# A gated linear-attention kernel on one core: two neighbouring tokens per partition, and the order of the engines written out

## The chip, the cores and the metric

The kernel runs on one core of a Trainium2 chip. A core has TensorE (PE, whose weight loads are shown apart as PEld), VectorE (DVE), ScalarE (ACT), GpSimd (POOL) and SyncE (SP, which here only issues DMAs), all with their own in-order instruction streams, joined by semaphores. The metric is device time in microseconds; lower is better. Three runs of the kernel before took 164.64, 166.47 and 166.83 us, a median of 166.47 us.

## The reference

Inputs r, k, v, w have shape (batch 4, heads 8, tokens 768, head size 48) in float32, u is (8, 48). For each batch and head a 48 x 48 state is carried over the tokens, and the result feeds a token-mixing MLP with 384 = 8 x 48 features and 64 hidden ones:

```python
for t in range(S):
    cur = np.einsum('bhd,bhe->bhde', u[None] * kt, vt)          # bonus for the token itself
    y[:, :, t] = np.einsum('bhd,bhde->bhe', rt, state + cur)
    state = wt[:, :, :, None] * state + np.einsum('bhd,bhe->bhde', kt, vt)
# x: y with heads joined, (4, 768, 384)
W_tok = scale * np.einsum('bsd,btd->bst', x @ w_q, x @ w_k)
mixed = np.einsum('bst,btd->bsd', W_tok, x)
out = np.maximum(mixed, 0.0) @ w_out
```

## The kernel before

The work is cut into 12 units, three to a batch element; a unit is two chunks of 128 tokens. Each chunk has one token per partition, and the free dimension holds the 8 heads of 48. The scan over tokens becomes matrix products: inside a chunk, the logarithms of w are summed over tokens by a triangular matmul; exponentials of these sums scale r (up to the token) and k (inverse); scaled r and k are transposed, multiplied into a 128 x 128 matrix A for each head, masked to its strict lower part, and multiplied with v. A bf16 state (SB) carries over from chunk to chunk.

Three stages follow one another for each unit. `prep` (lines 136 to 169) loads (line 125, eight DMAs of 192 KB from the SP queue, in each of which a row is the 48 floats of one token and head, 192 bytes), takes the logarithm on ACT (L142), the sums on PE, two exponentials of 128 x 768 on ACT (L148, L156), the chunk decays (L158), the scaled r on DVE (`RdS`, L162), the scaled k on POOL (`KdS`, L164) and a bf16 copy of v on ACT (L167). `back` (171 to 203) transposes r and k on PE into `psT`, copies them out (`RKT`, L179), makes A on PE and the masked `AmB` on DVE (L189), the products r·u·k on POOL (L194, L197), their reduction on DVE (`diag`, L199) and the bonus-weighted values `Vd` on POOL (L201). `scan` (205 to 258) takes for each chunk the state (`Sn` on PE, `SB` on DVE, L226) and the output (`Y` on PE, `X` = Y + Vd on DVE, L238), then transposes X (`XT`, L247) and projects it (`qk`, L256, L257). After a batch element's third unit `moe` (260 to 283) does the rest: `Tps`, six `mps` with a Relu on ACT (L272), six `fps` of three matmuls each, copied out by DVE and ACT in turn (L280, L282) and stored from the ACT queue.

The program is written unit by unit, `prep` of a unit ahead of `back` and `scan` of the one before, and a scheduler in the framework reorders each engine's instructions. Tile pools set how far engines can run apart: loads have four buffers each; in PSUM the tags `big` (sums, `psT`, A), `s` (`Sn`, `Y`) and `m` (the MLP) have two each. All matmuls go through the helper on line 55.

Of the kernel before, what the change touches and what calls it, by code (L numbers as in the profile page):

```python
# [25 lines left out]
def kernel(  # L26
# [14 lines left out]
    C = 128  # L41
    NCH = S // C
    NP = H // 2
    NU = S // (2 * C)
# [9 lines left out]
    def mm(o, l, rr, start=True, stop=True, sgc=True, trans=False):  # L54
        nc.tensor.matmul(o, l, rr, start=start, stop=stop,  # L55
                         skip_group_check=sgc, is_transpose=trans)

    nc.scalar.preload_act_table_set("natural_log_exp_and_others")

    consts = ctx.enter_context(tc.tile_pool(name="consts", bufs=1))  # L60
    U128 = consts.tile([C, C], BF16, tag="U128")
    make_upper_triangular(nc, U128, 1.0, diag=True)
    US128 = consts.tile([C, C], BF16, tag="US128")
    make_upper_triangular(nc, US128, 1.0, diag=False)
    ID128 = consts.tile([C, C], BF16, tag="ID128")
    make_identity(nc, ID128)
    ones = U128[:, C - 1:C]

    iota0 = consts.tile([C, 1], mybir.dt.int32, tag="iota0")
    nc.gpsimd.iota(iota0, pattern=[[0, 1]], base=0, channel_multiplier=1)  # L70
    iota1 = consts.tile([C, 1], mybir.dt.int32, tag="iota1")
    nc.gpsimd.iota(iota1, pattern=[[0, 1]], base=1, channel_multiplier=1)
    bias_px = consts.tile([C, 1], F32, tag="bpx")
    bias_mi = consts.tile([C, 1], F32, tag="bmi")
    bias_c = consts.tile([C, 1], F32, tag="bc")
    nc.scalar.activation(bias_px, iota0, ACT.Copy, bias=0.0, scale=MU)
    nc.scalar.activation(bias_mi, iota1, ACT.Copy, bias=0.0, scale=-MU)
    nc.gpsimd.memset(bias_c, MU * C)


# [3 lines left out]
    for i in range(NB):  # L84
        for lst, nm, e in ((LW, "logw", nc.gpsimd), (RdS, "RdS", nc.vector),
                           (KdS, "KdS", nc.gpsimd)):
            t = consts.tile([C, 2, NP, C], BF16, name=f"{nm}{i}", tag=f"{nm}{i}")
            e.memset(t, 0.0)
            lst.append(t)
        t = consts.tile([C, 2, H], F32, name=f"pt{i}", tag=f"pt{i}")  # L90
        nc.vector.memset(t, 0.0)
        PT.append(t)
# [8 lines left out]
    ld = ctx.enter_context(tc.tile_pool(name="ld", bufs=4))  # L101
# [6 lines left out]
    mout = ctx.enter_context(tc.tile_pool(name="mout", bufs=4))  # L108

    def mtile(shape, dtype, name):  # L110
        return ps.tile(shape, dtype, name=name, tag="m", bufs=2)

    def stile(shape, dtype, name):
        return ps.tile(shape, dtype, name=name, tag="s", bufs=2)
# [4 lines left out]
    def load(n):  # L119
        b, m = divmod(n, NU)  # L120
        G = {}
        for nm, ap in (("w", w), ("k", k), ("r", r), ("v", v)):
            t = ld.tile([C, 2, H, D], F32, name=nm + "G", tag=nm + "G")
            for c in range(2):
                nc.sync.dma_start(out=t[:, c], in_=ap[  # L125
                    b, :, ds((m * 2 + c) * C, C)].rearrange("h p d -> p h d"))
            G[nm] = t
        return G

    def chd(t):  # L130
        return t
# [4 lines left out]
    def prep(n, G):  # L136
        P = {}
        logw = LW[n % NB]
        Rd = RdS[n % NB]
        Kd = KdS[n % NB]  # L140
        pt = PT[n % NB]
        nc.scalar.activation(pad(logw), chd(G["w"]), ACT.Ln, bias=0.0, scale=LN_SCALE)  # L142
        cw1 = big([C, 2, 512], F32, "cw1")
        lw4 = pad(logw)
        for c in range(2):
            mm(cw1[:, c, 0:DM].rearrange("p (h d) -> p h d", d=D), US128, lw4[:, c])
# [58 lines left out]
    def scan(n, P, st):  # L205
# [8 lines left out]
        for cc in range(2):  # L214
            c = 2 * m + cc
            SB = st["S"]
            if c + 1 < NCH:
                Sn = stile([C, DM], F32, "Sn")
                if SB is not None:
                    mm(Sn, ID128, SB, start=True, stop=False)  # L220
# [114 lines left out]
```

## Time and profile before

| | |
|---|---|
| profiled execution, whole | 165.66 us |
| its span, first to last instruction | 163.9 us |
| PE busy | 104.8 us in 1196 matmuls |
| DVE busy | 99.2 us |
| POOL busy | 95.7 us |
| ACT busy | 80.9 us |
| loads on the SP queue | 18.98 MB in 100242 packets |
| stores on the ACT queue | 4.72 MB in 3456 packets |

Times are of one profiled execution, in microseconds, and means of one instruction in nanoseconds. In the page's rows of 40 slices each digit is the busy share of a fortieth of the span in tenths; the DMA row is the mean over 16 DMA engines. A row of the groups reads: line, engine, operation, out<-in, shapes, count, then busy time and mean of one, then the idle time of the engine just before them and what ended it. A row of the timeline begins with start and duration. A matmul's listed length includes its passage through the array, so neighbours overlap; the pace is seen from the time from start to start.

### The profile page before, as it was taken

To read this page: it belongs to the slowest core of one execution; us is meant where nothing else is said; L and a number is where in the kernel's file an instruction comes from. 1 tells how busy PE (TensorE), PEld (TensorE's weight loads), DVE (VectorE), ACT (ScalarE), POOL (GpSimd) and SP (SyncE) were. 2 spreads that over 40 slices of the span, in tenths; PEclk is the share of its full clock that TensorE was granted. 3 is DMA by queue.
4 is the path that set the end of the run, shared out by engine and by line. 5 is a ranking of instruction groups with operands and counts; after the bars stand their busy time and mean duration, and the time that the engine had idled before them with its cause. 6 is when DMAs were issued, how large, how long until landed. Compare 5 with 4: busy or idle time off the path is not lost.

```text
span 163.9 us, 3082 instructions
## 1 busy us (share of the span) xinstructions
PE 104.8 (64%) x1196; PEld 70.8 (43%) x1196; DVE 99.2 (61%) x124; ACT 80.9 (49%) x152; POOL 95.7 (58%) x72
## 2 busy tenths in 40 slices
PE   0305103752379488994958898886589949857690
PEld 0203003441257365674637366665344527734240
DVE  4020203645668997899889978899582696670030
ACT  3535420430155576775729757793766342303721
POOL 7931009999994999598696952949960940000000
PEclk9999999999999999998799999699975995765967
DMA  5999999999999990289989969999970331000034
GB/s 111 194 187 187 190 187 186 182 210 172 192 183 190 167 175 0 72 221 268 194 165 190 174 173 256 220 197 187 159 140 0 110 125 59 4 0 0 0 127 161
DMA packets 104512, 24.23 MB, mean 148 GB/s; under 512 B 101041, under 2 KB 104498, under 8 KB 104498
## 3 DMA queue, kind: packets, MB, share of 16 engines
q1 hardware_dynamic: 100242, 18.98, 75.0%
q10 hardware_dynamic: 3456, 4.72, 8.2%
q0 software_dynamic: 800, 0.34, 1.7%
q8 instruction: 9, 0.15, 0.4%
q14 instruction: 5, 0.04, 0.1%
HBM read 19.66 MB, written 4.72 MB: 149 GB/s over the span
## 4 chain that ended last, share of the span: by engine, by line
PE 29%; SPq 16%; POOL 15%; DVE 14%; issue 10%; ACT 7%; DMA 6%; ACTq 0%; POOLq 0%
SPq L125 15%; DMA rG<-in_r_dram 6%; DVE AmB L189 6%; PE fps L55 6%; POOL uk L197 5%; PE Y L55 5%; POOL uk L194 4%; PE qk L55 3%; PE psT L55 3%; DVE RKT L179 3%; PE cw L55 3%; POOL KdS L164 3%; POOL Vd L201 3%; PE Tps L55 3%; ACT XT L247 2%
## 5 line engine op out<-in xcount | busy, mean ns | idle before, releaser
L164 POOL TENSOR_TENSOR KdS<-kG,emcw 128x768 bf16<-128x768 f32 x12 | 21.1, 1758 | 18.9 <-ACT emcw L156 11.1
L189 DVE TENSOR_TENSOR AmB<-A,US 128x1024 bf16<-128x1024 f32 x24 | 28.3, 1219 | 4.4 <-PE A L55 4.3
L162 DVE TENSOR_TENSOR RdS<-rG,ecwx 128x768 bf16<-128x768 f32 x12 | 17.2, 1433 | 14.5 <-DMA rG<-in_r_dram 13.4
L197 POOL TENSOR_TENSOR uk<-uk,rG 128x768 f32<-128x768 f32 x12 | 24.3, 2028 | 0.5
L201 POOL TENSOR_TENSOR Vd<-VB,diag 128x768 bf16<-128x768 bf16 x12 | 18.4, 1532 | 10.0 <-DVE diag L199 6.0
L194 POOL TENSOR_TENSOR uk<-kG,ubc 128x768 f32<-128x768 f32 x12 | 21.7, 1810 | 1.7 <-DMA kG<-in_k_dram 1.7
L179 DVE COPY RKT<-psT 128x2048 bf16<-128x2048 bf16 x12 | 14.6, 1218 | 11.1 <-PE psT L55 11.1
L247 ACT COPY XT<-xt_ps 128x768 bf16<-128x768 bf16 x12 | 9.6, 798 | 20.8 <-PE xt_ps L55 20.6
L238 DVE TENSOR_TENSOR X<-Y,Vd 128x384 bf16<-128x384 f32 x24 | 13.2, 552 | 9.2 <-PE Y L55 5.9
L55 PEld LDWEIGHTS <-KdS 128*128 128x128 bf16 x176 | 13.7, 113 | 11.5 <-POOL KdS L164 9.4
L55 PE MATMUL Y<-VB,AmB 128*128 128x48 bf16 x192 | 10.7, 199 | 11.7 <-DVE AmB L189 9.8
L148 ACT ACTIVATE ecwx<-cw,bias_px 128x768 bf16<-128x768 f32 x12 | 10.8, 902 | 14.2 <-PE cw L55 14.2
L55 PEld LDWEIGHTS <-RKT 48*128 48x128 bf16 (+1 forms) x272 | 12.3, 105 | 10.7 <-DVE RKT L179 7.4
L55 PE MATMUL fps<-wout_sb,mixT 128*128 128x384 bf16 x72 | 15.9, 365 | 0.7 <-ACT osb L282 0.3
L55 PE MATMUL cw<-logw,US 128*128 128x384 bf16 x24 | 8.2, 438 | 12.5 <-ACT logw L142 12.5
L55 PEld LDWEIGHTS <-AmB 128*128 128x128 bf16 x192 | 8.4, 107 | 17.6 <-DVE AmB L189 14.8
L55 PE MATMUL psT<-ID,KdS 128*128 128x128 bf16 x96 | 9.4, 242 | 9.1 <-POOL KdS L164 9.1
L199 DVE TENSOR_REDUCE diag<-uk 128x16 f32<-128x768 f32 x12 | 11.4, 946 | 6.3 <-POOL uk L197 6.3
L280 DVE COPY osb<-fps 128x384 f32<-128x384 f32 x12 | 6.7, 554 | 14.0 <-PE fps L55 14.0
L167 ACT CAST VB<-vG 128x768 bf16<-128x768 f32 x12 | 10.0, 830 | 10.3 <-DMA vG<-in_v_dram 10.1
L55 PE MATMUL A<-RKT 48*128 48x128 bf16 x192 | 10.5, 235 | 6.2 <-DVE RKT L179 5.6
L142 ACT ACTIVATE logw<-wG 128x768 bf16<-128x768 f32 x12 | 10.1, 843 | 6.6 <-DMA wG<-in_w_dram 6.5
(54 smaller groups left out, 196.9 us busy)
## 6 DMA issues: line engine op xcount, KB each, us to landing
wG<-in_w_dram SPq DMA_DIRECT2D x24, 192.0 KB, 4.6
kG<-in_k_dram SPq DMA_DIRECT2D x24, 192.0 KB, 4.5
rG<-in_r_dram SPq DMA_DIRECT2D x24, 192.0 KB, 4.5
vG<-in_v_dram SPq DMA_DIRECT2D x24, 192.0 KB, 4.7
out_dram<-osb ACTq DMA_DIRECT2D x24, 192.0 KB, 2.0
wout_sb<-in_moe_w_out_dram POOLq DMA_DIRECT2D x1, 288.0 KB, 6.1
wq_f<-in_moe_w_q_dram SPq DMA_DIRECT2D x1, 96.0 KB, 4.1
wk_sb<-in_moe_w_k_dram POOLq DMA_DIRECT2D x1, 48.0 KB, 4.3
```

The costliest lines, as they stand in the source:

```text
L55: nc.tensor.matmul(o, l, rr, start=start, stop=stop, skip_group_check=sgc, is_transpose=trans)
L125: nc.sync.dma_start(out=t[:, c], in_=ap[b, :, ds((m * 2 + c) * C, C)].rearrange("h p d -> p h d"))
L162: nc.vector.tensor_tensor(pad(Rd), chd(G["r"]), ecwx.rearrange("p c (h d) -> p c h d", d=D), ALU.mult)
L164: nc.gpsimd.tensor_tensor(pad(Kd), chd(G["k"]), emcw.rearrange("p c (h d) -> p c h d", d=D), ALU.mult)
L179: nc.vector.tensor_copy(RKT, psT)
L189: nc.vector.tensor_tensor(AmB[:, c].rearrange("p q h t -> p h q t"), A, _rep(_rep(US128, 1, NP), 1, 2), ALU.mult)
L194: nc.gpsimd.tensor_tensor(uk, G["k"], _rep(ubc.rearrange("p (h d) -> p h d", d=D), 1, 2), ALU.mult)
L197: nc.gpsimd.tensor_tensor(uk, uk, G["r"], ALU.mult)
L199: nc.vector.tensor_reduce(diag, uk, axis=AX.X, op=ALU.add)
L201: nc.gpsimd.tensor_tensor(Vd, VB, _rep(diag, 3, D), ALU.mult)
L238: nc.vector.tensor_tensor(X[:, c], Y8, P["Vd"][:, cc].rearrange("p h d -> p (h d)"), ALU.add)
L247: nc.scalar.copy(XT[:, :, ds(m * 2 * C, 2 * C)], tp)
```

## The change

One load now brings a whole unit of a tensor: partition p holds the tokens 2p and 2p+1 of the unit's 256, so a row of the DMA is 2 x 48 floats, 384 bytes. There are four loads a unit instead of eight, with three buffers each instead of four.

The scan stays in that layout. A chunk q is now the half of the partitions from 64q on, and index j (0, 1) is the token of the pair. So the sums need two matmuls each, one for each j, with block-diagonal triangular matrices (`BI` with, `BS` without the diagonal), in three PSUM tiles `cw1`, `cw2`, `cw0`; A is made in 64-row pieces, 32 matmuls a unit instead of 16, `Sn` in 16 instead of 8, `Y` in 32 instead of 16. The exponentials are four of 128 x 384, and those for r stay in PSUM, where DVE reads them (`rdec`). The transposes write the tokens so that columns of a chunk are in the order (j, i); rows of Y and X come out in that order. The bonus-weighted values `Vd` are made in the load layout, and four DMAs a unit from SP (`vswap`, 64 partitions each, SBUF to SBUF) regroup them into `Vn` in the order of Y. X is then made by one DVE instruction for both chunks. The stores undo the order: two DMAs for each pair of chunks.

In PSUM `psT`, A, `Sn` and `Y` now share the two buffers of `big`, and everything else has the four of `m`.

The order of every engine is written out: each step has a number, a unit's steps are shifted by P = 7.42 for each unit, a batch element's MLP steps by the unit that ends it, and the program is issued in the order of the numbers, with the scheduler off. Three places show what moves.

On DVE, in the middle of the run, before (`SB2` are states, `Y8` outputs, `fps` a result of the MLP; numbers are buffers):

```order
L162 TENSOR_TENSOR RdS1_94<-rG_847,ecwx_857 128x16x48
L179 COPY RKT_895<-psT_878 128x2048
L226 TENSOR_TENSOR SB2_931<-Sn_925,pt0_90 128x384
L189 TENSOR_TENSOR AmB_897<-A_898,US128_64 128x2x4x128
L199 TENSOR_REDUCE diag_1279<-uk_1276 128x16
L189 TENSOR_TENSOR AmB_897<-A_908,US128_64 128x2x4x128
L238 TENSOR_TENSOR X_778<-Y8_933,Vd_923 128x384
L226 TENSOR_TENSOR SB2_953<-Sn_947,pt0_90 128x384
L162 TENSOR_TENSOR RdS2_102<-rG_995,ecwx_1005 128x16x48
L238 TENSOR_TENSOR X_778<-Y8_955,Vd_923 128x384
```

And now, one unit of the same part:

```order
L289 TENSOR_TENSOR SB2_752<-Sn_740,pt2_81 128x384
L246 TENSOR_REDUCE diag_773<-uk_592 128x8x2
L209 COPY RKT_851<-psT_756 128x2048
L325 TENSOR_TENSOR X_495<-Y_803,Vn_697 128x768
L182 TENSOR_TENSOR RdS0_71<-rG_395,cw0_800 128x8x48
L182 TENSOR_TENSOR RdS0_71<-rG_395,cw1_786 128x8x48
L226 TENSOR_TENSOR AmB_873<-A_853,MASK_58 128x2x4x128
L226 TENSOR_TENSOR AmB_873<-A_889,MASK_58 128x2x4x128
L289 TENSOR_TENSOR SB2_939<-Sn_920,pt3_85 128x384
```

X of a unit stands between the RKT copy of the next unit and the scaling of r of the one after; both masks of a unit come after the X of the unit before.

On PE, where the output Y begins, before (A, then Y):

```order
L55 LDWEIGHTS RKT_895
L55 MATMUL A_908<-RKT_895 128x128
L55 LDWEIGHTS AmB_897
L55 MATMUL Y8_933<-VB_729,AmB_897 128x48
L55 LDWEIGHTS RKT_895
L55 MATMUL Y8_933<-SB2_805,RKT_895 128x96
```

And now, from the last transpose of a unit over the sums of the next to the Y of the one before (a first and a last row of each kind, with their weight loads):

```order
L58 MATMUL psT_943<-ID128_59,KdS0_72 128x2x64
L58 LDWEIGHTS ID128_59
L58 MATMUL Sn_920<-SB2_939,ID128_59 128x384
L58 LDWEIGHTS BI_60
L58 MATMUL cw1_976<-logw1_74,BI_60 128x384
L58 MATMUL cw2_979<-Q2_62,logw1_74 128x2
L58 LDWEIGHTS BS_61
L58 MATMUL cw0_990<-logw1_74,BS_61 128x384
L58 LDWEIGHTS AmB_873
L58 MATMUL Y_993<-V2_749,AmB_873 128x48
```

Y, which followed A of its own chunk, now follows the transposes of the next unit and the sums of the one after that.

On ACT, at the start of the program, before:

```order
L142 ACTIVATE logw0_84<-wG_146 128x16x48
L148 ACTIVATE ecwx_164<-cw1_161,bias_px_78 128x768
L156 ACTIVATE emcw_177<-cw0_166,bias_mi_79 128x768
L158 ACTIVATE pt0_90<-cw0_166,bias_c_80 48x8 x2
L167 CAST VB_183<-vG_155 128x768
L142 ACTIVATE logw1_92<-wG_185 128x16x48
```

And now:

```order
L139 ACTIVATE logw0_70<-wG_192 128x16x48
L139 ACTIVATE logw1_74<-wG_202 128x16x48
L159 ACTIVATE em_243<-cw1_226,bias2_67 128x384
L159 ACTIVATE em_243<-cw2_229,bias3_68 128x384
L166 ACTIVATE cw0_240<-cw0_240,bias0_65 128x384
L166 ACTIVATE cw1_226<-cw1_226,bias1_66 128x384
L173 ACTIVATE pt0_73<-cw2_229,bias_c_69 48x4x2 x2
L139 ACTIVATE logw2_78<-wG_213 128x16x48
L193 CAST V2_254<-vG_200 128x768
L159 ACTIVATE em_303<-cw1_286,bias2_67 128x384
```

The logarithm of the second unit now stands ahead of the first unit's exponentials, and that of the third ahead of the first unit's cast of v.

On SP the loads of a unit follow the four swaps of the unit three before it, and on POOL a unit has u·k, times r, `Vd` of the unit before, `KdS`, in this order throughout. The diff, cut to its core:

```diff
     def load(n):
-        for nm, ap in (("w", w), ("k", k), ("r", r), ("v", v)):
-            t = ld.tile([C, 2, H, D], F32, name=nm + "G", tag=nm + "G")
-            for c in range(2):
-                nc.sync.dma_start(out=t[:, c], in_=ap[
-                    b, :, ds((m * 2 + c) * C, C)].rearrange("h p d -> p h d"))
+    def load(n, nm, ap):
+        src = ap[b, :, ds(m * C2, C2)]
+        t = ld.tile([C, H, D2], F32, name=nm + "G", tag=nm + "G")
+        nc.sync.dma_start(out=t, in_=src.rearrange("h (p j) d -> p h (j d)", j=2))
...
+    def sums(n):
+        for i, m0, m1 in ((1, BI, BS), (2, BI, BI), (0, BS, BS)):
+            cw = T["cw", n, i] = mtile([C, 512], F32, f"cw{i}")
+            od = cw[:, 0:DM].rearrange("p (h d) -> p h d", d=D)
+            mm(od, m0, lw4[:, 0], stop=False)
+            mm(od, m1, lw4[:, 1], start=False)
...
-        nc.scalar.activation(ecwx, cw1[:, :, 0:DM], ACT.Exp, bias=bias_px, scale=1.0)
+    def expr(n):
+        for j in range(2):
+            cw = T["cw", n, j][:, 0:DM]
+            nc.scalar.activation(cw, cw, ACT.Exp, bias=bias[j], scale=1.0)
...
+    def trR(n, j):
+        for hp in range(NP):
+            for jj in range(2):
+                mm(o[:, :, hp, ds(jj * HC, HC)], src[:, jj, hp], ID128, trans=True)
+    def amat(n, js):
+        A = big([C, 2, NP, C], F32, "A")
+        for hp in range(NP):
+            for q, hh in ((0, 0), (1, 1), (1, 0), (0, 1)):
+                mm(A[ds(q * HC, HC), hh, hp],
+                   RKT[ds(hh * 64, D), 1, q, hp, ds(js * HC, HC)],
+                   RKT[ds(hh * 64, D), 0, q, hp], start=(hp == 0))
+    def vswap(n):
+        Vn = bt.tile([C, 2, DM], BF16, name="Vn", tag="Vn")
+        for q in range(2):
+            for j in range(2):
+                nc.sync.dma_start(
+                    out=Vn[ds(j * HC, HC), q],
+                    in_=T["Vd", n][ds(q * HC, HC), j].rearrange("p h d -> p (h d)"))
+    def state(n):
+        for hp in range(NP):
+            for j in range(2):
+                for q in range(nq):
+                    mm(Sn[:, q, ds(hp * D2, D2)], T["Kd", n][ds(q * HC, HC), j, hp],
+                       T["V2", n][ds(q * HC, HC), j, ds(2 * hp, 2)].rearrange(
+                           "p h d -> p (h d)"), start=(hp == 0 and j == 0))
+    def ymat(n):
+        for h in range(H):
+            for js in range(2):
+                for q in range(2):
+                    mm(Y[:, q, ds(h * D, D)],
+                       T["AmB", n][ds(q * HC, HC), js, h // 2, h % 2],
+                       T["V2", n][ds(q * HC, HC), js, h], start=(h == 0 and js == 0))
+    def yev(n):
+        nc.vector.tensor_tensor(T["X", b][:, ds(2 * m, 2)], T["Y", n][:, :, 0:DM],
+                                T["Vn", n], ALU.add)
...
+    P = 7.420616340685398
+    steps = [
+        (-6.28, log, ()),
...
+        (24.22, qkev, ()),
+    ]
...
+    with tc.manual_schedule():
+        for _, _, fn in sorted(plan, key=lambda x: x[:2]):
+            fn()
```

More of the change, by code (lines that the diff above doesn't have):

```diff
@@ L84 @@
     for i in range(NB):
[L85 to L92, printed above, removed]
+        for lst, nm in ((LW, "logw"), (RdS, "RdS"), (KdS, "KdS")):
+            lst.append(consts.tile([C, 2, NP, C], BF16, name=f"{nm}{i}", tag=f"{nm}{i}"))
+        PT.append(consts.tile([C, 2, H], F32, name=f"pt{i}", tag=f"pt{i}"))
     u1 = consts.tile([1, DM], F32, tag="u1")
@@ L285 @@
[L285 to L305 removed]
+            mm(Tps, T["wk", b][:, c], T["X", b][:, c], start=(c == 0), stop=(c == NCH - 1))
```

504 lines of the change are left out of this document (327 added, 177 removed).

## The prediction

> **What bounds the kernel now.** I read the page first: shares, slices, queues.
>
> ```profile
> span 163.9 us, 3082 instructions
> PE 104.8 (64%) x1196; PEld 70.8 (43%) x1196; DVE 99.2 (61%) x124; ACT 80.9 (49%) x152; POOL 95.7 (58%) x72
> ...
> DVE  4020203645668997899889978899582696670030
> ...
> POOL 7931009999994999598696952949960940000000
> ...
> DMA  5999999999999990289989969999970331000034
> ...
> q1 hardware_dynamic: 100242, 18.98, 75.0%
> q10 hardware_dynamic: 3456, 4.72, 8.2%
> ```
>
> No engine is busy for two thirds of the span. The DMA row stands at 9 from the first to the thirtieth slice, with one gap; DVE and POOL reach 9 only from the fifteenth slice and the sixth. So loads feed the first 123 us, and what comes after runs dry from the left. The timeline shows the price of a load, and of the lead-in:
>
> ```profile
> 4.83 0.84 ACT L142 ACTIVATE logw<-wG 128x768 bf16<-128x768 f32 x1 [2.33 <-DMA wG<-in_w_dram]
> 9.56 2.04 SPq L125 DMA_DIRECT2D kG<-in_k_dram  x2
> 13.26 0.84 ACT L142 ACTIVATE logw<-wG 128x768 bf16<-128x768 f32 x1 [1.30 <-DMA wG<-in_w_dram]
> 117.89 1.46 SPq L125 DMA_DIRECT2D vG<-in_v_dram  x2
> ```
>
> One tensor of a unit (two DMAs, 2048 rows of 192 bytes, 393 KB) takes 2.04 us of queue when loads run back to back, a unit 4 x 2.04 = 8.2 us, twelve units 98 us. The last is issued at 118 us; the rest of the time went into SP's waits and stores. The pace of units shows in one tile:
>
> ```profile
> L179 DVE COPY RKT<-psT x12: 1210/1218/1225, 27.2 to 141.2; 128x2048 bf16<-128x2048 bf16 x12
> 146.43 0.56 DVE L238 TENSOR_TENSOR X<-Y,Vd 128x384 bf16<-128x384 f32 x1 [0.45 <-PE Y L55]
> ```
>
> Eleven steps in 114.0 us: 10.4 us a unit, where DVE works 99.2/12 = 8.3 us. Three parts, then: 27 us until the first RKT, eleven units, and 163.9 - 147.0 = 16.9 us from the last X to the end.
>
> **The change, part by part.** What DVE will do in a unit is priced by these groups (busy, mean ns):
>
> ```profile
> L189 DVE TENSOR_TENSOR AmB<-A,US 128x1024 bf16<-128x1024 f32 x24 | 28.3, 1219 | 4.4 <-PE A L55 4.3
> L162 DVE TENSOR_TENSOR RdS<-rG,ecwx 128x768 bf16<-128x768 f32 x12 | 17.2, 1433 | 14.5 <-DMA rG<-in_r_dram 13.4 <-ACT ecwx L148 1.0
> L238 DVE TENSOR_TENSOR X<-Y,Vd 128x384 bf16<-128x384 f32 x24 | 13.2, 552 | 9.2 <-PE Y L55 5.9 <-POOL Vd L201 3.1
> L199 DVE TENSOR_REDUCE diag<-uk 128x16 f32<-128x768 f32 x12 | 11.4, 946 | 6.3 <-POOL uk L197 6.3
> L226 DVE TENSOR_TENSOR SB<-Sn,pt 128x384 bf16<-128x384 f32 x20 | 11.0, 549 | 0.2
> L280 DVE COPY osb<-fps 128x384 f32<-128x384 f32 x12 | 6.7, 554 | 14.0 <-PE fps L55 14.0
> ```
>
> RKT 1.22, two masks 2.44, reduction 0.95, states 20/12 x 0.549 = 0.92. RdS becomes two products of 384 elements with one operand in PSUM; no row has that pair, the nearest is X (same size, PSUM and SBUF): 2 x 0.55 = 1.10 against 1.43. X becomes one instruction of 768; by the line through 384 (0.552) and 1024 (1.219) it takes 0.95. Together 7.58 us, and one osb copy a unit 0.55: 8.13 us. DVE's work falls by 0.1 us only, so the gain must come from its waits.
>
> *Loads.* A row is now 384 bytes, a tensor of a unit 1024 rows. If a row costs what it did, a tensor takes 1.02 us; if bytes count, 2.04. I take the middle, 1.5, since 1365 bytes a packet on the store queue (8.2% x 16 x 163.9/3456 = 62 ns) against 189 on the load queue (19.6 ns) shows a cost that grows with bytes, but more slowly. A unit's loads: 6.0 us; stores 8.2% x 163.9/12 = 1.1; swaps 197 KB a unit, 0.6 by the store's price and 1.0 by the load's, taken 0.8. Sum 7.9 us (5.8 to 10.3). [...] No trace here has a 384-byte row.
>
> *The swap.* Four DMAs a unit bring Vd into the old row order. On SP they wait for Vd, and the next unit's four loads stand behind them. Vd(n) ends some 3 us into a period (reduction at 1.5, then 1.5 on POOL), and X(n) reads it in the next period at 4: 10 us of cover at a period of 9. Landing took 2.0 to 4.7 us before:
>
> ```profile
> rG<-in_r_dram SPq DMA_DIRECT2D x24, 192.0 KB, 4.5
> vG<-in_v_dram SPq DMA_DIRECT2D x24, 192.0 KB, 4.7
> out_dram<-osb ACTq DMA_DIRECT2D x24, 192.0 KB, 2.0
> ```
>
> So I cost it at nothing; without the cover it is its landing on each unit. The loads behind it have three units of buffers.
>
> *TensorE.* It gains 16 A, 8 state and 16 Y matmuls a unit, each on 64 rows of the array or fewer, and two more sums.
>
> ```profile
> 28.44 1.03 PE L55 MATMUL A<-RKT 48*128 48x128 bf16 x16 [1.00 <-DVE RKT L179]
> 142.72 0.62 PE L55 MATMUL A<-RKT 48*128 48x128 bf16 x16
> 80.64 0.61 PE L55 MATMUL psT<-ID,KdS 128*128 128x128 bf16 x8
> 67.72 0.36 PE L55 MATMUL Y<-VB,AmB 128*128 128x48 bf16 x8
> 67.56 0.41 PEld L55 LDWEIGHTS <-AmB 128*128 128x128 bf16 x8
> 68.04 1.14 PE L55 MATMUL fps<-wout_sb,mixT 128*128 128x384 bf16 x6
> ```
>
> Start to start, with one matmul's own length taken off: psT (0.61-0.22)/7 = 56 ns for 128 columns; A, whose neighbours lie on different row halves, (0.62-0.22)/15 = 27 ns, half of it, so halves overlap; at 28 us the same A went at 54 ns, at half rate. fps (1.14-0.33)/5 = 0.162 us for 384 columns; Y 24 ns, its weight loads 0.41/8 = 51. With overlap a unit is: sums 6 x 0.162 + 0.2 = 1.2, transposes 0.9, A 32 x 27 = 0.86, Y 32 x 24 to 51 = 0.8 to 1.6, states' part 0.3, Sn 0.6, xt 0.33, qk 0.6, and the batch's 30 wide matmuls 10 x 0.162 = 1.65: 7.3 to 8.1 us.
>
> *What DVE still waits for.* The PSUM tiles of the transposes, A, Sn and Y share two buffers in turn. From the end of a unit's second mask (0): transposes 0.9 and the state's matmul 0.16 to 1.1, sums to 2.3, Y 0.8 to 1.4 (its pace taken at 24 to 43 ns), its eight state matmuls 0.3 (42 ns each, psT's 56 x 96/128), latency 0.2: 3.6 to 4.2. DVE is done with state, reduction, state and RKT at 0.55+0.95+0.55+1.22 = 3.3. It waits 0.3 to 0.9 for Y; with the semaphores and the change between array forms I take 0.85 (0 to 1.4). So a period is 7.58+0.85 = 8.43 us, and 9.0 with the osb copy. That exceeds POOL's 95.7/12 = 8.0, TensorE's 8.1 and the queues' 7.9. ACT:
>
> ```profile
> L148 ACT ACTIVATE ecwx<-cw,bias_px 128x768 bf16<-128x768 f32 x12 | 10.8, 902 | 14.2 <-PE cw L55 14.2
> L272 ACT ACTIVATE mixT<-mps 128x384 bf16<-128x384 f32 x24 | 10.8, 489 | 2.1 <-PE mps L55 1.7
> L167 ACT CAST VB<-vG 128x768 bf16<-128x768 f32 x12 | 10.0, 830 | 10.3 <-DMA vG<-in_v_dram 10.1
> ```
>
> Two exponentials of 768 become four of 384: 4 x 0.49 - 2 x 0.90 = +0.16; 80.9/12 + 0.16 = 6.9 us. Hidden.
>
> *Lead-in.* ACT now takes log(1) ahead of the first exponentials and log(2) ahead of unit 0's cast and unit 1's exponentials, so each waits for a later w. First w at 4.8 as before; w of unit 2 is eight tensors on, 4.8 + 8 x 1.5 = 16.8. Then log 0.84, cast 0.83, four exponentials 1.96, RdS(1) 1.1, both masks of unit 0 2.4: 23.9 us. This is DMA time; its bounds are 20 and 28.
>
> *The sum.* Masks of unit 0 end at 23.9; ten periods of 8.43: 84.3; six osb copies among them 3.3; two batches in which fps waits for a PSUM buffer until RdS is done, 0.5 each: 1. Last unit: 0.55+0.95+0.55+1.22+0.85+0.95, masks 2.44, osb 0.55, state 0.55, 0.3 for Y's state part, X 0.95: 9.9. Tail 16.9 as before, plus 0.5 for three fps of the batch before that now stand ahead of the last xt: 17.4. Span 139.8. The profiled execution took 165.66 us, 1.8 more than its span; that makes 141.6. Against the median of the runs (166.47) the profiled one is 0.8 low, so I say 142 us.
>
> **Rivals.**
>
> A, bytes count. [...] Loads end at 98 + 11 swaps of 1.0 + 10 of stores = 120 us; from there cast, masks, copies, Y and X some 8, tail 17.4, 1.8: 148. For it: slices at 9. Against: the packet prices above.
>
> B, TensorE binds. If 64-row matmuls don't overlap in these forms, A costs 32 x 56 = 1.8, Sn 0.9 and Y 1.6: 9.3 us a unit; each of about eight changes between array forms may add up to a matmul's length, 0.2: to 10.9. At the middle, 10.1, it is 142 + 10 x 1.1 = 153 (145 to 161). For it: Y's weight loads at 51 ns. Against: A at 27. [...]
>
> C, no wait for Y. DVE runs full: ten periods less 0.85 each, 133.5.
>
> D, slower: the half rate. At 28 us TensorE ran A at 54 ns. If it stays there, 7.3 becomes 14.6 a unit and it binds: 142 + 10 x 5.6 = 198. The old time is passed at a period of 11.5, when nearly 6 tenths of its work go at half rate. Against: the full rate was there once it was busy, and it will be busier.
>
> E, the swap takes the place of the removed wait: behind queued loads it lands 12 us after its issue, period 11.2, 164 us, no change. Against: 2.0 to 4.7.
>
> **Numbers.** Forecast 0.50, A 0.12, B 0.13, C 0.14, D 0.05, E 0.06. Range 130 to 156: it takes in A, C, most of B and the bounds of lead-in and wait; D, E and B's end are left out. A measurement can tell 2% (3.3 us; the three runs shown spread over 2.2). The first four are faster, 0.89; E 0.06; D 0.05.
>
> **What would show it.** RKT's steps: 8.5 to 9.2 us. DVE's idle time ahead of X, put down to Y, about 0.85 a unit; RdS at 0.55 and X at 0.95. Load packets of 384 bytes, half as many, DMA slices below 9 once the lead-in is over. If slices stay at 9, A; if DVE waits for A and Y everywhere with TensorE full, B; X waiting for Vn, E; A at 54 ns late in the span, D. Wrong altogether if ACT's order costs more than the lead-in.

## The result, and the profile after

The changed kernel took 147.87 us (median of four runs, 147.4 to 150.44), the kernel before 165.56 us beside it (164.39 to 166.83): a ratio of 0.887, with a 95% interval of 0.875 to 0.900. Faster, and inside the range, but 6 us above the 142 that were forecast. The profiled execution is the longest of the four, 150.44 us with a span of 148.7, so its parts read somewhat long. Medians here and below are over all executions, ratios and intervals over the undisturbed ones alone (of the kernel before sometimes only two), so a difference of two medians is good to about 2 us.

The page of the changed kernel, with the rows that answer to those of before:

```profile
span 148.7 us, 4118 instructions
...
PE 100.9 (68%) x1684; PEld 66.7 (45%) x1684; DVE 92.5 (62%) x138; ACT 81.8 (55%) x174; POOL 88.1 (59%) x85
...
DVE  5002000045769889898899896997989989760210
...
POOL 7603400899999597989596987949596803000000
...
DMA  4999990019298949679796967969856310248074
...
q1 hardware_dynamic: 53762, 21.24, 54.1%
```

The SP queue's packets, the regrouping's included, are about half as many and hold the DMA engines 54% of the span where they held 75%. DVE runs mostly at 8 to 9 tenths from the thirteenth slice to the thirty-third. But before that DVE stands at 0 from the fifth slice to the eighth, POOL in the sixth and seventh, and the DMA row has a hole of two slices.

The groups, the tile and the timeline of DVE, from one X to the next in mid-run (start, duration, and the idle time before in brackets):

```profile
L325 DVE TENSOR_TENSOR X<-Y,Vn 128x768 bf16<-128x768 f32 x12 | 11.5, 958 | 7.3 <-PE Y L58 4.0 <-PE Tps L58 1.5 <-PE A L58 1.1
```

```profile
L209 DVE COPY RKT<-psT x12: 1214/1215/1225, 32.7 to 124.0; 128x2048 bf16<-128x2048 bf16 x12
```

```profile
59.96 0.96 DVE L325 TENSOR_TENSOR X<-Y,Vn 128x768 bf16<-128x768 f32 x1 [0.81 <-PE Y L58]
60.84 1.01 DVE L182 TENSOR_TENSOR RdS<-rG,cw 128x384 bf16<-128x384 f32 x2
61.77 2.35 DVE L226 TENSOR_TENSOR AmB<-A,MASK 128x1024 bf16<-128x1024 f32 x2
64.03 0.55 DVE L289 TENSOR_TENSOR SB<-Sn,pt 128x384 bf16<-128x384 f32 x1
64.50 0.94 DVE L246 TENSOR_REDUCE diag<-uk 128x16 f32<-128x768 f32 x1
65.42 0.56 DVE L289 TENSOR_TENSOR SB<-Sn,pt 128x384 bf16<-128x384 f32 x1
65.89 1.22 DVE L209 COPY RKT<-psT 128x2048 bf16<-128x2048 bf16 x1
67.38 0.96 DVE L325 TENSOR_TENSOR X<-Y,Vn 128x768 bf16<-128x768 f32 x1 [0.27 <-PE Y L58]
...
130.82 0.96 DVE L325 TENSOR_TENSOR X<-Y,Vn 128x768 bf16<-128x768 f32 x1 [0.42 <-PE Y L58]
```

Eleven RKT steps take 91.3 us, 8.30 each, where they took 10.4. The first RKT stands at 32.7 us, later than before (27.2). From the end of the last X to the end of the span it is 148.7 - 131.78 = 16.9 us, as before. So the units gave 23 us; the lead-in took more than 5 of them back, and the stretch from the last RKT to the last X, 7.8 us where it was 5.8, another 2. POOL's timeline shows where the lead-in lost its time:

```profile
5.54 0.82 POOL L446 MEMSET KdS<- 128x256 bf16 x3
13.59 0.68 POOL L451 PARTITION_BROADCAST ubc<-u  x1 [7.24 <-issue]
14.12 1.06 POOL L454 DMA_DIRECT2D wq_f<-in_moe_w_q_dram  x1
15.20 0.78 POOL L455 DMA_DIRECT2D wk_sb<-in_moe_w_k_dram  x1
15.96 0.77 POOL L456 DMA_DIRECT2D wout_sb<-in_moe_w_out_dram  x1
26.36 1.79 POOL L232 TENSOR_TENSOR uk<-kG,ubc 128x768 f32<-128x768 f32 x1 [9.63 <-issue]
```

```profile
17.00:26.00 9.00, 0.00 (x0) 0.00 (x0) 0.00 (x0) 0.00 (x0) 0.00 (x0) 1.00 0.64 133
```

POOL stands still for 7.24 us ahead of the broadcast that spreads u over the partitions, and for 9.63 us after it (behind the issue of three weight loads), and the second row (busy time of PE, PEld, DVE, ACT, POOL from 17 to 26 us) says that all five stood still with it. u's own load was issued at 1.2 us, and ACT read at 9.96 us a w whose load was issued behind it, at 4.7; the broadcast began only at 13.59, so the first gap is no wait for that. The same stood in the trace of before, on POOL, under other names:

```profile
15.90 0.68 POOL L293 PARTITION_BROADCAST ubc<-u  x1 [6.21 <-ACT ecwx L148]
24.40 3.23 POOL L164 TENSOR_TENSOR KdS<-kG,emcw 128x768 bf16<-128x768 f32 x2 [7.82 <-DMA kG<-in_k_dram]
```

Those two gaps were put down to ACT's `ecwx` and to a load of k, and I passed them by as waits of the loads. (There u's load was issued only at 7.4 us, so a part of the 6.21 may be its landing.)

### The profile page after: what moved, and what is told of

It reads as the page before. It is cut to its first block, busy times and chain, and to the rows that moved or that the text cites. A ratio compares the mean times of both kernels' runs of the same rounds, so it can differ in the third digit from the quotient of the medians.

```text
span 148.7 us, 4118 instructions
## 1 busy us (share of the span) xinstructions
PE 100.9 (68%) x1684; PEld 66.7 (45%) x1684; DVE 92.5 (62%) x138; ACT 81.8 (55%) x174; POOL 88.1 (59%) x85
## 3 DMA queue, kind: packets, MB, share of 16 engines
q1 hardware_dynamic: 53762, 21.24, 54.1%
## 5 line engine op out<-in xcount | busy, mean ns | idle before, releaser
L159 ACT ACTIVATE em<-cw,bias 128x384 bf16<-128x384 f32 x24 | 12.8, 577 | 29.2 <-PE cw L58 29.2
L226 DVE TENSOR_TENSOR AmB<-A,MASK 128x1024 bf16<-128x1024 f32 x24 | 28.5, 1217 | 0.3 <-PE A L58 0.2
L253 POOL TENSOR_TENSOR Vd<-V,diag 128x768 bf16<-128x768 bf16 x12 | 17.7, 1474 | 17.9 <-DVE diag L246 12.8
L58 PEld LDWEIGHTS <-KdS 64*128 64x128 bf16 (+1 forms) x256 | 11.6, 104 | 22.2 <-POOL KdS L189 17.7
L58 PE MATMUL psT<-ID,KdS 128*128 128x128 bf16 x96 | 8.3, 237 | 17.4 <-POOL KdS L189 17.4
L189 POOL TENSOR_TENSOR KdS<-kG,em 128x768 bf16<-128x768 f32 x12 | 19.6, 1636 | 0.3 <-ACT em L159 0.2
L182 DVE TENSOR_TENSOR RdS<-rG,cw 128x384 bf16<-128x384 f32 x24 | 12.1, 547 | 10.8 <-ACT cw L166 10.8
L325 DVE TENSOR_TENSOR X<-Y,Vn 128x768 bf16<-128x768 f32 x12 | 11.5, 958 | 7.3 <-PE Y L58 4.0
L58 PE MATMUL cw<-logw,BI 128*128 128x384 bf16 x36 | 11.4, 374 | 4.9 <-ACT logw L139 4.9
L289 DVE TENSOR_TENSOR SB<-Sn,pt 128x384 bf16<-128x384 f32 x20 | 11.1, 554 | 4.0 <-PE Sn L58 2.9
L166 ACT ACTIVATE cw<-cw,bias 128x384 f32<-128x384 f32 x24 | 12.3, 558 | 0.2
```

Source lines behind the costliest of these rows:

```text
L58: nc.tensor.matmul(o, l, rr, start=start, stop=stop, skip_group_check=True, is_transpose=trans)
L159: nc.scalar.activation(em[:, j], T["cw", n, 1 + j][:, 0:DM], ACT.Exp, bias=bias[2 + j], scale=-1.0)
L166: nc.scalar.activation(cw, cw, ACT.Exp, bias=bias[j], scale=1.0)
L182: nc.vector.tensor_tensor(pad(Rd)[:, j], jhd(T["r", n])[:, j], T["cw", n, j][:, 0:DM].rearrange("p (h d) -> p h d", d=D), ALU.mult)
L189: nc.gpsimd.tensor_tensor(pad(T["Kd", n]), jhd(T["k", n]), hd(T["em", n]), ALU.mult)
L226: nc.vector.tensor_tensor(T["AmB", n][:, js].rearrange("p q h t -> p h q t"), T["A", n, js], _rep(_rep(MASK[:, js], 1, NP), 1, 2), ALU.mult)
```

## The experiments

Each ratio is to the kernel before, run beside it on the same chip; its medians there were 166.0 to 167.0 us.

**u spread by the load.** The broadcast is replaced by a load whose source has a stride of zero over the partitions.

```diff
-        nc.sync.dma_start(out=u1, in_=u.rearrange("h d -> (h d)"))
-        nc.gpsimd.partition_broadcast(ubc, u1)
+        nc.sync.dma_start(out=ubc, in_=_rep(u.rearrange("h d -> (h d)"), 0, C))
```

> The changed kernel, with u spread over the partitions by the load itself instead of by POOL's PARTITION_BROADCAST. Theory K: the two idle stretches on POOL around that instruction (7.2 us ahead of it, 9.6 us behind it, both put down to 'issue') belong to it; without it POOL goes from its memsets (6.4) and three DMA issues (2.6) to the first uk at about 10 us instead of 26.4, KdS of unit 0 is there at 15 instead of 31.6, and the first RKT, at 32.7 before, comes at 17 to 19. All else as it was: 133 us (131 to 136). Rival W: the second stretch belongs to the three weight loads issued from POOL right ahead of it; then 9.6 us of it stay and the first stretch alone goes: 140 us.

Measured: 137.12 us, ratio 0.836 (0.820 to 0.852). POOL, then DVE, then the RKT tile in its trace:

```profile
8.51 1.79 POOL L231 TENSOR_TENSOR uk<-kG,ubc 128x768 f32<-128x768 f32 x1
```

```profile
14.30 1.02 DVE L181 TENSOR_TENSOR RdS<-rG,cw 128x384 bf16<-128x384 f32 x2 [11.31 <-ACT cw L165]
...
21.70 1.03 DVE L181 TENSOR_TENSOR RdS<-rG,cw 128x384 bf16<-128x384 f32 x2 [3.28 <-ACT cw L165]
22.65 2.35 DVE L225 TENSOR_TENSOR AmB<-A,MASK 128x1024 bf16<-128x1024 f32 x2
```

```profile
L208 DVE COPY RKT<-psT x12: 1212/1215/1225, 17.2 to 110.4; 128x2048 bf16<-128x2048 bf16 x12
```

Both gaps are gone, and what now holds the lead-in is the wait that the prediction had counted: exponentials in ACT's order behind later loads of w. The masks of unit 0 end at 25.0 us; 23.9 were predicted. That edit alone is worth 10.8 us between the medians of the changed kernel with and without it.

**The same edit in the kernel before.**

> The kernel before, with the same edit. Theory K: KdS of unit 0 comes at 10 us instead of 24.4 and the first RKT at about 13 instead of 27.2, but a tensor's load still takes 2.04 us, so that the queue (98 us of loads, 13 of stores) ends its loads at 112 instead of 119: 158 us (155 to 161). If the broadcast is not what POOL waited for: 165 us as it was.

Measured: 160.34 us, ratio 0.968 (0.951 to 0.985). The stall cost the kernel before some 5 to 6 us, a little less than the middle of what was expected, and more than that in the changed one. The loads did not end earlier than before, against my expectation: in the profiled execution the last were issued at 120 us.

**Rows of 192 bytes.** All else as changed: each tensor of a unit comes in two DMAs, one for each token of the pair.

```diff
-        nc.sync.dma_start(out=t, in_=src.rearrange("h (p j) d -> p h (j d)", j=2))
+        for j in range(2):
+            nc.sync.dma_start(out=t[:, :, ds(j * D, D)],
+                              in_=src.rearrange("h (p j) d -> j p h d", j=2)[j])
```

> The changed kernel, with each tensor of a unit loaded by two DMAs of 192-byte rows (one for each token of the pair) into the same tile; nothing else differs. Theory R: a row costs much the same whatever its length here, so a tensor takes 2.04 us again instead of 1.2 to 1.3, a unit's queue time is 8.2 + 1.1 + 0.8 = 10.1 us, more than the 8.3 us at which units now follow one another; from the fourth unit on the queue binds: 154 to 157 us. Rival A (bytes count): the same time as the changed kernel, 148 us, and the same DMA share.

Measured: 169.64 us, ratio 1.038 (1.020 to 1.057), beyond both. Its queue and DVE's longest waits:

```profile
q1 hardware_dynamic: 103682, 21.24, 63.7%
```

```profile
DVE X L327 <- DMA Vn<-Vd: 18.3, 5, 5.1
DVE diag L248 <- POOL uk L241: 13.2, 1, 13.2
DVE RdS L184 <- DMA rG<-in_r_dram: 11.5, 1, 11.5
```

X waits five times, 18.3 us in all, for the regrouped values: what rival E described, in the kernel with the narrow rows. (Each tensor also takes two DMAs here instead of one; rows and number of DMAs were not tried apart.)

**Without the regrouping**, at 384 and at 192 bytes; X takes Vd as it lies, so these kernels leave out bringing the bonus values to their own tokens.

```diff
-        Vn = bt.tile([C, 2, DM], BF16, name="Vn", tag="Vn")
-        for q in range(2):
-            for j in range(2):
-                nc.sync.dma_start(...)
-        T["Vn", n] = Vn
+        T["Vn", n] = T["Vd", n].rearrange("p c h d -> p c (h d)")
```

> The changed kernel without the regrouping: X takes Vd as it is, so the bonus rows are added to the wrong tokens; the four DMAs a unit are left out. My prediction's view: they are covered by a period of slack and the time stays, 147 to 148 us. Rival E: X waits for the swap, or the loads behind it on SP do; then 3 us or more go: 144 us or less.

Measured: 148.07 us, ratio 0.906 (0.893 to 0.919). The regrouping cost the changed kernel nothing that can be measured.

> The changed kernel with rows of 192 bytes (two DMAs for each tensor of a unit) and without the four DMAs a unit that regroup Vd: X takes Vd in the load order, so the regrouping is left out. With 192-byte rows and the regrouping the time was 169.6 us, and DVE waited 18.3 us for Vn. Theory S (with a full queue the regrouping stands behind loads and becomes the wait): without it 155 to 160 us. Rival R (the price of the rows alone makes that time, and the wait for Vn only stands in place of a wait for loads): 165 to 170 us, with the 18 us now put down to loads.

Measured: 148.05 us, ratio 0.892 (0.886 to 0.899), below both expectations. Without the regrouping, narrow rows cost nothing here that these runs can tell: 148.05 against 148.07. With it they cost 22 us (169.64 against 147.87). But both of these kernels still have the stall at the start, in which the queue brings in three units with nothing else to do. So I took the stall away from both:

> The changed kernel with u spread by the load, with rows of 192 bytes (two DMAs for each tensor of a unit) and without the regrouping (X takes Vd in the load order, so the regrouping is left out). With PARTITION_BROADCAST still there the same kernel took 148.05 us, as much as with 384-byte rows (148.07). Theory N (rows don't matter once the regrouping is gone): 136 to 139 us, as with 384-byte rows. Rival R2 (before, the loads had a head start while POOL stood still at the start; without it the narrow rows bind, at 1.65 to 2.0 us for a tensor of a unit, 6.6 to 8.2 us a unit beside 0.9 of stores): DVE waits for r or for the logarithms' w in more than the first two units, RKT steps of 8.9 us or more, 141 to 147 us.

> The changed kernel with u spread by the load and without the regrouping (X takes Vd in the load order, so the regrouping is left out); rows are 384 bytes. It stands against 137.1 us with the regrouping, and against 146.2 us for the same kernel with 192-byte rows. Theory Z (the regrouping lies beside other work also when the start has no stall, and the row width is worth the whole difference to 146.2): 136 to 138.5 us, queue share of the loads about 55%. Rival Y (its four transfers a unit, 0.6 us each on SP's queue among the loads of the first units, now cost): 132 to 135 us, RKT of the fourth unit at 42 us or earlier where it was at 44.5.

Measured: 146.24 us with 192-byte rows (ratio 0.895, 0.886 to 0.905) and 134.85 us with 384 (0.818, 0.795 to 0.841). The two intervals do not meet. The stretch from 45 to 105 us of the one with 192-byte rows, and then of the one with 384 (busy time of PE, PEld, DVE, ACT, POOL, then TensorE's granted clock, 1.00 being full speed, DMA share, GB/s):

```profile
45.00:105.00 60.00, 49.59 (x935) 33.84 (x936) 50.39 (x64) 42.56 (x93) 45.43 (x28) 1.00 0.99 201
```

```profile
45.00:105.00 60.00, 55.76 (x1005) 37.92 (x1006) 54.92 (x72) 45.95 (x101) 47.40 (x29) 0.97 0.64 168
```

With narrow rows the DMA share is 0.99, and DVE works 50.4 of 60 us; with wide rows it is 0.64, and DVE works 54.9. What the units wait for shows on ACT, where each begins with the logarithm of w (narrow rows, then wide):

```profile
ACT logw L140 <- DMA wG<-in_w_dram: 33.4, 12, 10.8
```

```profile
ACT logw L138 <- DMA wG<-in_w_dram: 13.2, 4, 6.8
```

With narrow rows every one of the twelve logarithms waits for its load, with wide rows four do. Without a stall the row width is worth 11.4 us. The regrouping takes some 2 of them back by the medians: 137.12 against 134.85, where the intervals overlap and theory and rival are not told apart (the fourth RKT came at 42.5 us).

**The order left to the scheduler**, in the changed layout with u by the load.

```diff
-    with tc.manual_schedule():
-        for _, _, fn in sorted(plan, key=lambda x: x[:2]):
-            fn()
+    for _, _, fn in sorted(plan, key=lambda x: x[:2]):
+        fn()
```

> The changed kernel with u spread by the load, but the engines' order left to the framework's scheduler, which takes the written steps in their order and may reorder them; the layout, the swap and the shared PSUM buffers stay. It stands against the same kernel with the order as written, 137.1 us, whose RKT steps take 8.5 us. Theory L (the layout carries the gain: fewer load packets and one X a unit, and the written order is only one of several good ones): 135 to 141 us, RKT steps of 8.3 to 8.8 us. Rival O (the order written out carries a good part: with another order DVE waits again for A, Y or the exponentials): 145 us or more, RKT steps of 9.2 us or more, with DVE's idle time ahead of the masks, of X or of RdS 0.7 us a unit above the written order's.

Measured: 186.98 us, ratio 1.127 (1.120 to 1.134); 50 us slower than the written order, and slower than the kernel before. Theory L falls. A wait of ACT, and then two of the groups of the page:

```profile
ACT XT L340 <- PE xt_ps L58: 50.4, 10, 8.8
```

```profile
L188 POOL TENSOR_TENSOR KdS<-kG,em 128x768 bf16<-128x768 f32 x12 | 19.6, 1636 | 46.8 <-ACT em L158 46.8
...
L208 DVE COPY RKT<-psT 128x2048 bf16<-128x2048 bf16 x12 | 14.7, 1223 | 22.4 <-PE psT L58 22.4
```

ACT waits 50 us for the transposes of X with the exponentials of a later unit behind it; KdS waits for those, RKT for KdS, and X of the next unit comes after RKT. In the written order the same XT waits 6.2 us, since X of a unit comes a period later, between the RKT of the next and the scaling of the one after. TensorE's granted clock was 0.815 in that execution against 0.955. But that execution was the shortest of the four (185.6 us; the others took 186.7 to 187.4 at 0.88), so a clock of 0.815 instead of 0.88 added nothing that shows; what the step from 0.88 to 0.955 is worth was not separated.

**The order on the old layout.** One token per partition, 192-byte rows, 128-row matmuls, no regrouping, all exponentials into SBUF; the order numbers, the shared PSUM buffers and one X a unit of the changed kernel, and u by the load. Its core:

```diff
-        t = ld.tile([C, H, D2], F32, name=nm + "G", tag=nm + "G")
-        nc.sync.dma_start(out=t, in_=src.rearrange("h (p j) d -> p h (j d)", j=2))
+        t = ld.tile([C, 2, H, D], F32, name=nm + "G", tag=nm + "G")
+        for c in range(2):
+            nc.sync.dma_start(out=t[:, c], in_=ap[
+                b, :, ds((m * 2 + c) * C, C)].rearrange("h p d -> p h d"))
...
-        (13.27, vswap, ()),
```

> The layout of before (one token per partition, 192-byte rows, eight loads a unit, 128-row matmuls, both exponentials into SBUF, Vd used as it is made) with the engines' order written out by the changed kernel's numbers, its PSUM buffers and one X a unit; u is spread by the load. It is the fourth corner of a square: layout of before under the scheduler 160.3 us, changed layout under the scheduler 187.0, changed layout in the written order 137.1. Theory G (the written order carries the whole gain and the layout none): DVE's work is 0.33 us a unit more than in the changed layout (one RdS of 1.43 us where there were two of 0.55), RKT steps of 8.6 to 9.0 us, 137 to 143 us. Rival H (the layout is needed for the gain: with loads of 8.2 us a unit the queue binds again): RKT steps of 9.5 us or more, DVE waiting for r or for the exponentials after w, 150 us or more.

Measured: 146.26 us, ratio 0.896 (0.888 to 0.904), between the two. With it there is a square, all four with u by the load (us):

| | framework's scheduler | written order |
|---|---|---|
| layout of before | 160.3 | 146.3 |
| changed layout | 187.0 | 137.1 |

On the old layout the written order is worth 14 us by the medians (12 by the ratios), but the two kernels of that row also differ in the PSUM buffers, in the depth of the load buffers and in having one X a unit or two, so this is the price of the order together with these. On the changed layout the order is all that differs, and it is worth 50. The layout is worth 9 more in the written order and loses 27 under the scheduler. At 146.3 the old layout stands level with the changed one at 192-byte rows without regrouping (146.2), and the DMA share is near 1 in both (1.14 and 0.99 from 45 to 105 us), so the 9 us could be the wide rows less the regrouping. That is not shown: in this kernel DVE is nearly full as well, 55.1 of 60 us, where the other had 50.4:

```profile
45.00:105.00 60.00, 49.37 (x661) 34.62 (x659) 55.10 (x55) 41.36 (x90) 49.29 (x27) 0.87 1.14 195
```

What the 64-row pieces and the sums left in PSUM are worth where loads don't bind was not tried. What fills DVE is RdS, which here reads SBUF on both sides. RdS in this kernel, and POOL's products beside it:

```profile
L180 DVE TENSOR_TENSOR RdS<-rG,ex x12: 1519/1748/2537, 19.6 to 118.5; 128x768 bf16<-128x768 f32 x12
```

```profile
58.89 2.28 DVE L180 TENSOR_TENSOR RdS<-rG,ex 128x768 bf16<-128x768 f32 x1
```

```profile
58.55 1.81 POOL L227 TENSOR_TENSOR uk<-kG,ubc 128x768 f32<-128x768 f32 x1
60.44 2.40 POOL L234 TENSOR_TENSOR uk<-uk,rG 128x768 f32<-128x768 f32 x1
```

In the kernel before, the same instruction on the same shapes took 0.95 us at the least, 1.01 in the median and 2.97 at the most:

```profile
L162 DVE TENSOR_TENSOR RdS<-rG,ecwx x12: 948/1014/2970, 9.1 to 128.0; 128x768 bf16<-128x768 f32 x12
```

In the written order it falls beside POOL's work each time and both stretch, RdS to 1.5 to 2.5 us and the product behind it from 1.81 to 2.40. In the rows above the product that was running keeps its 1.81, RdS ends 0.8 us after it, and the next one takes 0.6 longer, as if the two took turns; no row shows the cause. In the changed layout, where one operand lies in PSUM, two halves take 2 x 0.55, and POOL's products stay at 1.81.

**Neighbours on the same rows of the array.** Only the order of A's and Y's matmuls changes.

```diff
-            for q, hh in ((0, 0), (1, 1), (1, 0), (0, 1)):
+            for q, hh in ((0, 0), (1, 0), (0, 1), (1, 1)):
...
-        for h in range(H):
-            for js in range(2):
-                for q in range(2):
+        for q in range(2):
+            for h in range(H):
+                for js in range(2):
```

> The changed kernel with u spread by the load, and A's and Y's matmuls in another order: neighbours now lie on the same 64 rows of the array where they lay on different ones; the work is the same. It stands against 137.1 us. Theory V (pieces on different parts of the array overlap, and that is why A went at 13.6 ns and Y at 12.6 ns from start to start): A at 27 ns or more, Y at 25 ns or more, so 0.4 us more for 32 pieces of A and 0.4 us more for 32 of Y in a unit; both lie between DVE's masks and X, so RKT steps of 9.0 to 9.3 us and 143 to 147 us. Rival N (neighbours don't matter, or DVE has room for it): A and Y as before, or slower without effect, 136 to 139 us.

Measured: 138.25 us, ratio 0.831 (0.823 to 0.840). TensorE's timeline in the changed kernel, and then with the new order:

```profile
58.91 0.57 PE L58 MATMUL Y<-V,AmB 64*128 64x48 bf16 x32
...
59.86 0.42 PE L58 MATMUL A<-RKT 48*64 48x128 bf16 x16
```

```profile
60.80 0.89 PE L58 MATMUL Y<-V,AmB 64*128 64x48 bf16 x32
...
62.34 0.42 PE L58 MATMUL A<-RKT 48*64 48x128 bf16 x16
```

Y slows from 0.57 to 0.89 us, 10 ns a piece. That fits pieces on different rows that overlap; but in the new order neighbours of Y also add into the same output columns, one after the other, and this was not tried apart. A does not slow, although half of its neighbours now share rows; those still write different halves of the output's partitions, and which of the two counts was not tried. DVE's waits for Y rose from 4.4 to 6.5 us in the whole span, about 2 us, which the time can't tell from none. So Y's pace depends on the order of neighbours, as V says, and the price was N's.

**ACT's order at the start.** The logarithms of units 1 and 2 behind the decays of the unit before.

```diff
-            at(t0 + dt, lambda n=n, fn=fn, a=a: fn(n, *a))
+            t = t0 + dt
+            if fn is log and n in (1, 2):
+                t = t0 - P + 3.2
+            at(t, lambda n=n, fn=fn, a=a: fn(n, *a))
```

> The changed kernel with u spread by the load, and on ACT the logarithms of units 1 and 2 put behind the decays of the unit before, so that the first exponentials wait for no later w. Theory Q (in the lead-in ACT's order behind later loads of w is what sets the start of the masks): the products RdS of unit 1 come at about 16.5 us where they came at 21.7, the masks of unit 0 start at 17 to 18.5 us where they started at 22.65, and the time is 131 to 133 us. Rival M (the loads as a whole set the lead-in, so that what starts earlier waits for data later): the first masks earlier, but the twelfth RKT not before 109 us, and 136 to 138 us.

Measured: 137.71 us, ratio 0.822 (0.814 to 0.829). The first RKT came at 14.9 us instead of 17.2, the twelfth at 109.9 instead of 110.4, which is rival M. POOL, the SP queue and DVE show who took it:

```profile
18.85 1.47 POOL L252 TENSOR_TENSOR Vd<-V,diag 128x768 bf16<-128x768 bf16 x1
```

```profile
22.98 1.64 SPq L133 DMA_DIRECT2D vG<-in_v_dram  x1
24.72 3.15 SPq L259 DMA_DIRECT2D Vn<-Vd  x4
```

```profile
29.33 0.96 DVE L324 TENSOR_TENSOR X<-Y,Vn 128x768 bf16<-128x768 f32 x1 [4.28 <-DMA Vn<-Vd]
```

Vd of unit 0 is ready at 20.3 us, its regrouping is issued at 24.7 behind the loads of unit 3, and X waits 4.3 us. (The text on the change puts a unit's loads behind the regrouping of the unit three before it; it is four.) So I also put those loads behind it, and the logarithm of unit 3 like the others:

```diff
+        if n == 3:
+            tl = 13.28
```

> The changed kernel with u spread by the load and the start rearranged twice: on ACT the logarithms of units 1 to 3 stand behind the decays of the unit before, and on SP the four loads of unit 3 stand behind the regrouping of unit 0's Vd. With the first alone the time stayed at 137.7 us and X of unit 0 waited 4.3 us for Vn, whose transfer was issued at 24.7 us behind those loads, though Vd was ready at 20.3. Theory Q2 (the start is a chain of orders, and with both links loosened the earlier start stays): X of unit 0 at 24.5 to 26 us where it was at 29.3, the twelfth RKT at 105.5 to 107.5 where it was at 109.9, 133 to 135 us. Rival M2 (loads that start later make a later unit wait as much): X of unit 0 earlier, but the twelfth RKT not before 109, 137 to 138 us.

Measured: 138.32 us. X of unit 0 came at 26.4, near what was expected, and the next units gave it back (only the order of the waits is read here):

```profile
38.00 0.96 DVE L324 TENSOR_TENSOR X<-Y,Vn 128x768 bf16<-128x768 f32 x1 [3.37 <-DMA Vn<-Vd]
```

The wait for Vn moved to unit 1, and one RdS waited 5.6 us for r, which no RdS did in the kernel with u by the load. The twelfth RKT came at 112.5. That fits M2. From the start to about the fourth unit the order of arrival on one queue sets the pace, and moving one step forward moves the wait to another; from there DVE does (busy 54.1 of the 60 us from 45 to 105 with u by the load): from the fourth RKT to the twelfth in that kernel, 65.9 us or 8.24 a unit. Neither of the two rearranged starts differs from 137.1 us by more than its runs spread.

## Why the prediction was right, and where it was not

The sign and the range held, and DVE binds in mid-run, as was said (0.27 us idle in the 7.42 from X to X above). The reason given, that the load queue lets go, held in part. The kernel with narrow rows and without the regrouping took the same 148.05 us, so the wide rows were needed here only to carry the regrouping. Nor was the kernel before held by its queue alone: the same narrow rows in the written order went at (124.1 - 23.1)/11 = 9.18 us a unit, by the starts of the first and the twelfth RKT, where before they went at 10.4. The rest of the gain goes with the written order and what came with it, for which the forecast had no term.

By its own three terms, in the profiled span: masks of unit 0 end at 38.8 us (36.47 + 2.35) where 23.9 stood, +14.9; from there to the end of the last X 93.0 where 98.5 stood, -5.5; tail 16.9 where 17.4 stood, -0.5. 139.8 + 8.9 = 148.7. That the forecast came within 6 us is in part luck: a lead-in that was 15 us too short stood against periods that were 5.5 us too long.

- **Lead-in: the step that failed.** I read the first 27 us of before as loads and ACT's order, and the bounds 20 and 28 came from loads alone. The trace of before had POOL standing still for 6.2 us ahead of PARTITION_BROADCAST and for 7.8 us behind it. POOL's row, which the prediction shows, has 1, 0, 0 in its fourth to sixth slices; the text says that POOL reaches 9 only from the sixth (it is there in the second, and again from the seventh), and does not ask what the three slices were. The releasers printed at the gaps were no cause: `ecwx` is no input of the broadcast, and the first of the two KdS had its factor `emcw` by 8.4 us and, without the broadcast, ran at 9.35, so that its k was there too. In the changed kernel without it the masks end at 25.0, so the counting of loads and logarithms was right to 1.1 us, and the missing term was 14 us (38.8 less 25.0). The 7.24 us ahead of the broadcast and the 9.63 behind it went with the same edit; no row here shows what passes in either.
- **The period: too long by 0.6 us.** 8.30 us from RKT to RKT, below the 8.5 to 9.2 that were to show it; ten periods, six copies and two waits had made 8.9. The work itself was sized right instruction by instruction (RdS 0.547, X 0.958, masks 1.217), but I added listed durations, and the next instruction starts 0.08 to 0.09 us before the listed end (0.02 after the reduction): from X at 59.96 to X at 67.38 the durations add to 7.59, the steps from start to start, less the 0.27 of waiting, to 7.15. That is 0.44 us a unit, and 0.6 against the prediction's own prices (7.76 with two states), since a row of two instructions holds an overlap already. The smaller wait for Y, next, saved more; waits for Sn (2.9 us in the span), which had no term, took about that back.
- **The wait for Y: smaller.** 0.85 a unit was taken. DVE stood 7.3/12 = 0.6 ahead of X, 0.33 of it put down to Y. Y's 32 pieces took 0.57 us where I had 0.8 to 1.6, because I took no overlap from the neighbours that the written order of loops gives (0.89 with the other order of loops, inside what I had); for A, with the passage of 0.22 taken off as in the prediction, it is 13 ns where 27 stood. Rival B's condition (no overlap) is the opposite of what the trace shows (13 ns). That a change between array forms costs anything was my estimate, in B and as a part of the 0.85; no run shows it by itself. At the one from the sums to Y some 0.1 us are left over (0.42 us from the last sums' start, 58.49, to Y's, less two sums of 0.162), half of what B allowed.
- **Loads.** 1.5 us for a tensor were taken between 1.02 and 2.04; back to back they took 1.15:

```profile
13.93 1.15 SPq L134 DMA_DIRECT2D vG<-in_v_dram  x1
```

  So a row costs little more than it did (1.15 us for 1024 rows against 2.04 for 2048), and rival A is out. The step from 192 to 384 bytes, with one DMA where there were two, took the time from 2.04 to 1.15 and 11.4 us off the kernel without a stall or the regrouping. But in the kernel as changed the row width alone gave nothing (148.05 against 148.07): the stall hid it. It was worth its 22 us there only because the regrouping stands on the same queue.
- **The regrouping at nothing: right**, with 384-byte rows (148.07 without it), on a landing of 2.5 us. Rival E's mechanism is real: with 192-byte rows it took 18 us of waits. It was one step of row width away, which I had not said.
- **The order.** I had no term for it; it stood in the forecast as waits that go. The square shows that with its buffers and the single X it carries 12 to 14 us on the old layout, and that the new layout as the scheduler ordered it was slower than the kernel before.
- **ACT.** Its exponentials of 384 took 0.58 and 0.56 us where I took 0.49 from Relu: 0.3 us more a unit, hidden as predicted (81.8 us of 148.7).
- **C and D.** Without a copy in it, the period in mid-run was C's in size, 7.42 us where C had 7.58, but by overlap of instructions and not because the wait for Y had gone. The half rate of D stood only at the start: the first 32 pieces of A, at 34.8 us, took 1.07 us, (1.07-0.22)/31 = 27 ns each, and from 43.8 us on 16 of them 0.42, 13 ns.

## What to carry to other kernels

An idle stretch whose printed releaser is no input of what starts, or was done long before, is a term by itself (here 14 us of lead-in): look which instruction stands at its end, and price that before what the stretch is said to wait for. Here the wider DMA row paid where each unit waited for its load (146.24 against 134.85 us) and not where the stall hid the loads (148.05 against 148.07), and the regrouping on the same queue was free with wide rows and cost 18.3 us of waits with narrow ones; so cost both at the filling of the queue that the change leaves. When instructions on one engine follow each other, add steps from start to start (7.15 us on DVE here), not listed durations (7.59).

## What had not been expected of the hardware

- One PARTITION_BROADCAST on POOL stood between gaps of 7.24 and 9.63 us without a row; a load with a source stride of zero did the same work and took 10.8 us off the changed kernel, 5 to 6 off the one before.
- Thirty-two matmuls of 64 rows by 48 columns passed in 0.57 us with neighbours on different rows of the array and in 0.89 with neighbours on the same rows that also add into the same columns.
- A VectorE product with both inputs in SBUF took 0.95 us at the least and 1.5 to 2.5 beside GpSimd products, which stretched from 1.81 to 2.40; with one input in PSUM the two halves kept 0.54 to 0.56 each and those products 1.79 to 1.82.
